# The logits' PSUM bank joins the pool of all products: eight shared banks in place of seven and one

## The chip, the cores and the metric

The kernel runs on one core of a Trainium2 chip. The metric is device time in microseconds (us). The engines are TensorE (PE; its weight loads are PEld), VectorE (DVE), ScalarE (ACT), GpSimd (POOL) and SyncE (SP), which issues most DMAs. Products of TensorE land in PSUM, which has eight banks of 128 partitions by 512 float32 words; DVE or ACT reads them out.

## What is computed

Two layers, one behind the other, in float32. The first mixes 8 batches of 2496 tokens of 256 channels by a filter in the frequency domain; the second sends each token to one of 8 experts.

```python
X = np.fft.rfft(x, axis=1)                      # x: 8 x 2496 x 256
y = np.fft.irfft(X * (filt_r + 1j * filt_i)[None], n=2496, axis=1)
x = y.reshape(19968, 256)
logits = x @ w_gate                             # 8 experts
expert_idx = np.argmax(logits, axis=1)
probs = softmax(logits); gate_w = probs[np.arange(N), expert_idx]
for e in range(8):                              # the rows of expert e
    h = np.maximum(x_sorted[lo:hi] @ w1[e], 0.0)     # 256 -> 1024
    y_sorted[lo:hi] = h @ w2[e]                      # 1024 -> 256
out = gate_w[:, None] * y_sorted[inv_perm]
```

## The kernel before

**The transform.** A sequence of 2496 = 39 x 64 tokens is transformed by small matrices. For each batch `stage_a` (table `tas`, tile `fin` into `zo`, stored to `zd`) makes the transform of length 39; `stage_b` (table `tbs`) that of length 64, with the filter applied on DVE while the product is read: into `ys` by one multiplication, into `yw` by two of half the partitions, all three reading the bank; then `ys` and `yw` are added, on DVE or POOL. `stage_c` (table `tcs`, from `ys` into `uo`, stored to `ud`) and `stage_d` (table `tds`, from `fin` loaded out of `ud`, into `yo`) go back. Batch 0 keeps its intermediate values on the chip (`first_a`, `turn_z`, `first_c`, `turn_u`).

**The logits.** The rows of `yo` are turned (`turn_y`), multiplied by the gate weights into the PSUM tile `lt`, and copied out into `ls`. Batches 0 to 2 do this in `logits`, up to eight rows of tokens at a time, and turn the result back in `turn_logits`; batches 3 to 7 do it in `block_logits`, with blocks of 32 channels, and `block_back`. A side stream, `route`, then finds expert and place of each token with small DVE instructions, and POOL scatters the rows to DRAM (`rows`); `tile_map` decides which tile of rows belongs to which expert.

**The experts.** Tiles of 512, 256 or 128 rows are loaded (`xg`), turned on DVE (`xT`), multiplied by `w1t` into `hT` and by `w2t` (or `w2s`, weights that stay) into the result `ys`, which POOL scatters to the output. Large tiles use products "by quarters": sums of blocks (`sums`, `wsum`, `hsum`, `tsum`) with seven products in place of eight, whose results DVE adds into `hT` as it reads the banks; ACT applies the ReLU.

**PSUM.** All products but the logits' ask `bank()` for a tile in the pool `ps` with seven banks. The logits' tile `lt` has a pool of its own, `psr`, with one bank, which is part of the transform's set of pools (`fft`) and is given up with it, when the last batch has been routed; nothing opens a PSUM pool after that.

**The order of the work.** The order of instructions is decided when the program is built, by `Order`: it keeps a clock for every engine (`t["tensor"]` and so on), with estimates for each operation, the times at which tiles are done (`ready`) and at which buffers come free (`Slots.free`). The main loop takes the next step for TensorE from the open steps of the transform (`wait_of`) and from two streams of expert products (`when`), and prefers what it holds to be startable within 0.2 us. Both ask for a free bank:

```python
banks = ps.free("bank") if f[3] < 0.9 else max(ps.free("bank"), ps.free("bank", 1) - 0.85)
return max(0.0, max(nc.ready(*needs), banks) - t["tensor"])
```

`ps.free("bank", 1)` is the time at which a second bank comes free. Steps of logits ask in this way too, though `lt` lies in the other pool. Which bank a product gets is decided by the same clock, since `ps` is marked as live: `tile` takes the one that is freed first by the plan. `either` gives a read of a bank to DVE or ACT, whichever ends it first by the plan. Loads and stores are issued on SP when the plan's TensorE clock has reached their time (`more_loads`, `flush`, `prefetch`). On the chip, each instruction waits by semaphores for what it really needs, in the order that the plan has set for its engine.

Of the kernel before, what the change touches and what calls it, by code (L numbers as in the profile page):

```python
# [10 lines left out]
F32 = mybir.dt.float32  # L11
# [5 lines left out]
PSUM = bass.MemoryType.PSUM  # L17
DRAM = bass.MemoryType.DRAM

P = 128  # L20
S = 2496
D = 256
E = 8
# [9 lines left out]
NG = 22  # L33
TP = NB * N1
# [5 lines left out]
CT = 32  # L40
# [253 lines left out]
def kernel(  # L294
# [19 lines left out]
    def open_pool(stack, name, bufs, **named):  # L314
        return nc.pool(stack.enter_context(tc.tile_pool(name=name, bufs=bufs, **named)), bufs)
# [9 lines left out]
    for b in range(B):  # L325
        GROUPS.append([])
        for rows, most in WANT[b]:
            n = min(most, max(0, ((b + 1) * S - (N - left) - E * (rows - 1)) // rows))
# [22 lines left out]
    tau0 = perm.tile([1, 32], F32, name="tau0")  # L351
    prow = perm.tile([P, 1], I32, name="prow")
    need = perm.tile([1, 1], I32, name="need")
    ps = open_pool(ctx, name="ps", bufs=7, space=PSUM)

    fft = ctx.enter_context(ExitStack())
    cst = open_pool(fft, name="cst", bufs=1)
    sb = open_pool(fft, name="sb", bufs=2)
    psr = open_pool(fft, name="psr", bufs=1, space=PSUM)

    tas = cst.tile([TP, TK], F32, name="tas")
    tbs = cst.tile([P, P], F32, name="tbs")
# [33 lines left out]
    def bank():  # L396
        return ps.tile([P, 512], F32, tag="bank", name="bank")
# [12 lines left out]
    def evac(o, i, n):  # L410
        either(i, n, lambda: nc.vector.tensor_copy(o, i), lambda: nc.scalar.copy(out=o, in_=i))
# [281 lines left out]
    def block_logits(b, c):  # L693

        n = CH[c][1]
        yt = yts.pop((b, c))
        lt = psr.tile([P, 2, E * NG], F32, tag="lt", name="lt").rearrange("p i w -> p (i w)")[:, :n * CT]
        for r in range(2):
            for q in range(4):
                j = 4 * r + q  # L700
                mm(lt[q * CT:(q + 1) * CT], lhsT=wb[:, j, :], rhs=yt[:, :, j * CT:(j + 1) * CT], start=(r == 0), stop=(r == 1))
        ls = outs["s", b, c] = sb.tile([P, 4 * CT], F32, tag="ls", name="ls", bufs=1)[:, :n * CT]
        evac(ls, lt, n * CT)
# [8 lines left out]
    def logits(b, g):  # L712

        js = range(min(4, NG // 2 - 4 * g))
        w = len(js) * CT
        both = [yts.pop((b, c)) for c in range(2 * g, min(2 * g + 2, len(CH)))]
        pair = [both[j // 2][:, j % 2].rearrange("p (i h) q -> p i h q", i=2) for j in js]
        lt = psr.tile([P, 2, E * NG], F32, tag="lt", name="lt")[:, :, :TP]
        for dh in range(DH):
            for j in js:  # L720
                mm(lt[j * CT:(j + 1) * CT], lhsT=wg[:, dh, :], rhs=pair[j][:, :, dh, :],
                   start=(dh == 0), stop=(dh == DH - 1))
        ls = sb.tile([P, 4, D], F32, tag="yt", name="ls")[:, :2, :TP]
        evac(ls[:w], lt[:w], 2 * TP)
        outs["l", b] = (g, w, ls)
# [849 lines left out]
```

## Time and profile before

| | |
|---|---|
| median of 3 runs | 1476.66 us (1476.07 to 1478.16) |
| profiled execution | 1478.19 us, span 1476.5 us |
| mean granted clock of TensorE | 0.995 |
| bytes moved by DMA | 278.19 MB, 188 GB/s in the mean |

The profile is of one execution. Its span goes from the first to the last instruction of the program; the execution's own time is 1.7 us longer. A group of instructions is named by output and inputs, `bank<-ys,tcs`, with the buffers' numbers left out, so all banks of `ps` are `bank`. All lines are L246, since a helper issues everything. A wait is put down to the instruction that released it.

### The profile page before, as it was taken

The page shows a single profiled execution, that of the slowest core. Times are in us where ns is not written, and L with a number is a line of the kernel's source. Part 1 is how long each engine was busy: PE and PEld are TensorE (multiplying, and loading weights), DVE is VectorE, ACT ScalarE, POOL GpSimd, SP SyncE. Part 2 cuts the span into 40 slices and gives each one's busy share as a digit, 9 for nine tenths or more (in the row PEclk, how much of TensorE's full clock was granted, in tenths as well). Part 3 has the DMA queues.
Part 4 walks back from the last instruction along what each step waited for, and adds up shares of the span by engine and source line. Part 5 has one row for each costly group of instructions (what it writes and reads, how often), then busy time and mean ns, then how long its engine had stood idle before and what let it go on. Part 6 is the DMA issues. An engine that isn't in the chain of part 4 may idle for free.

```text
span 1476.5 us, 25693 instructions
## 1 busy us (share of the span) xinstructions
PE 1440.1 (98%) x7828; PEld 1147.0 (78%) x7828; DVE 848.7 (57%) x1819; ACT 480.6 (33%) x1004; POOL 822.0 (56%) x1213
## 2 busy tenths in 40 slices
PE   8998998999999999999999999999999999999998
PEld 6543656877677777776787778879999998999997
DVE  4667579235866675457665465567878775431110
ACT  4554452333332232322222232223232322223332
POOL 4434445635555654655465656858989878831111
PEclk9999999999999999999999999999999999999999
DMA  9759889795985585556544735556655425456661
GB/s 269 230 193 340 280 291 299 253 258 185 321 206 167 172 260 151 131 162 229 156 119 132 214 93 148 153 177 188 173 173 167 133 71 137 135 189 176 174 190 43
DMA packets 216383, 278.19 MB, mean 188 GB/s; under 512 B 124131, under 2 KB 163708, under 8 KB 216245
## 3 DMA queue, kind: packets, MB, share of 16 engines
q1 hardware_dynamic: 197125, 233.19, 53.2%
q0 software_dynamic: 19120, 43.33, 8.4%
q8 instruction: 66, 1.08, 0.3%
q14 instruction: 72, 0.59, 0.1%
HBM read 196.45 MB, written 80.64 MB: 188 GB/s over the span
## 4 chain that ended last, share of the span: by engine, by line
PE 85%; DVE 6%; DMA 4%; issue 3%; ACT 1%; POOL 0%; SPq 0%; DVEq 0%; POOLq 0%; ACTq 0%
PE bank L246 83%; DMA fin<-in_x_dram 2%; PE lt L246 2%; DVE hT L246 1%; DVE yw L246 1%; DVE ys L246 1%; DMA fin<-ud 1%; DMA fin<-zd 1%; DMA zd<-zo 1%; POOL out_dram L246 0%; DVE take L246 0%; ACT hT L246 0%; SPq L246 0%; DMA w1t<-in_moe_w_dram 0%; DMA xg<-rows 0%
## 5 line engine op out<-in xcount | busy, mean ns | idle before, releaser
L246 DVE TENSOR_TENSOR hT<-bank,hT 128x512 f32<-128x512 f32 (+1 forms) x504 | 301.9, 626 | 181.4 <-PE bank L246 101.2
L246 PE MATMUL bank<-w2t,hT 128*128 128x256 f32 (+1 forms) x1984 | 388.6, 350 | 1.6 <-DVE hT L246 1.6
L246 PEld LDWEIGHTS bank<-w2t,hT 128*128 128x128 f32 x1984 | 334.5, 190 | 49.9 <-issue 9.6
L246 PE MATMUL bank<-xT,w1t 128*128 128x256 f32 (+1 forms) x1728 | 314.9, 328 | 0.3 <-DVE hT L246 0.3
L246 POOL DMA_INDIRECT out_dram<-ys,ng x161 | 160.0, 994 | 252.5 <-ACT ys L246 121.5
L246 PEld LDWEIGHTS bank<-xT,w1t 128*128 128x128 f32 x1728 | 264.6, 191 | 33.1 <-issue 9.9
L246 ACT ACTIVATE hT<-hT 128x1024 f32<-128x1024 f32 (+1 forms) x144 | 135.5, 960 | 399.8 <-DVE hT L246 387.4
L246 POOL DMA_INDIRECT rows<-yo,row x176 | 181.9, 1033 | 70.8 <-POOL yo L246 31.3
L246 ACT ACTIVATE ys<-bank,ng 128x256 f32<-128x256 f32 x102 | 48.4, 475 | 287.4 <-PE bank L246 231.7
L246 PE MATMUL bank<-sums,wsum 128*128 128x256 f32 (+1 forms) x576 | 135.7, 358 | 1.5 <-DVE hT L246 1.5
L246 PE MATMUL bank<-w2s,hT 128*128 x592 | 132.9, 380 | 1.3 <-ACT hT L246 1.3
L246 POOL TENSOR_TENSOR wsum<-w1t 128x256 f32<-128x256 f32 x72 | 60.1, 835 | 114.5 <-PE bank L246 96.7
L246 PEld LDWEIGHTS bank<-w2s,hT 128*128 128x128 f32 x592 | 110.2, 190 | 15.8 <-ACT hT L246 2.0
L246 PEld LDWEIGHTS bank<-sums,wsum 128*128 128x128 f32 x576 | 100.3, 190 | 21.6 <-issue 11.3
L246 DVE STREAM_TRANSPOSE xT<-xg 128x512 f32<-128x512 f32 (+2 forms) x126 | 57.5, 494 | 57.7 <-PE bank L246 56.9
L246 PE MATMUL bank<-ys,tcs 128*128 128x512 f32 x140 | 73.8, 613 | 7.6 <-DVE yw L246 4.2
L246 DVE TENSOR_TENSOR ys<-bank,ht 128x512 f32<-128x512 f32 x80 | 54.9, 686 | 44.3 <-PE bank L246 38.0
L246 PE MATMUL bank<-fin,tds 120*128 120x512 f32 (+1 forms) x168 | 77.1, 580 | 3.1 <-DMA fin<-ud 2.6
L246 PE MATMUL bank<-fin,tas 117*120 117x512 f32 x154 | 75.5, 608 | 4.2 <-DMA fin<-in_x_dram 3.3
L246 PE MATMUL bank<-fin,tbs 128*128 128x512 f32 x140 | 72.7, 607 | 2.3 <-DMA fin<-zd 2.2
L246 ACT ACTIVATE hT<-bank 128x128 f32<-128x128 f32 (+1 forms) x191 | 57.2, 303 | 53.9 <-PE bank L246 45.3
L246 PE MATMUL bank<-xT,wsum 128*128 128x256 f32 (+1 forms) x288 | 68.8, 362 | 1.1 <-DVE yw L246 0.9
(171 smaller groups left out, 1778.9 us busy)
## 6 DMA issues: line engine op xcount, KB each, us to landing
w1t<-in_moe_w_dram SPq DMA_DIRECT2D x126, 512.0 KB
w2t<-in_moe_w_dram SPq DMA_DIRECT2D x68, 512.0 KB
fin<-in_x_dram SPq DMA_DIRECT2D x39, 512.0 KB
fin<-zd SPq DMA_DIRECT2D x35, 512.0 KB
ud<-uo SPq DMA_DIRECT2D x35, 512.0 KB
fin<-ud SPq DMA_DIRECT2D x35, 512.0 KB
zd<-zo SPq DMA_DIRECT2D x35, 480.0 KB
xg<-rows SPq DMA_DIRECT2D x112, 128.0 KB
```

What stands on the lines that cost most here:

```text
L246: return real(*args, **named)
```

## The change

The pool `ps` gets eight banks. The pool `psr` is dropped, and both logits functions take their tile from `bank()`. In `logits` the two halves of the tile now begin 256 words apart in place of 176.

```diff
-    ps = open_pool(ctx, name="ps", bufs=7, space=PSUM)
+    ps = open_pool(ctx, name="ps", bufs=8, space=PSUM)
...
-    psr = open_pool(fft, name="psr", bufs=1, space=PSUM)
...
-        lt = psr.tile([P, 2, E * NG], F32, tag="lt", name="lt").rearrange("p i w -> p (i w)")[:, :n * CT]
+        lt = bank()[:, :n * CT]
...
-        lt = psr.tile([P, 2, E * NG], F32, tag="lt", name="lt")[:, :, :TP]
+        lt = bank().rearrange("p (i w) -> p i w", i=2)[:, :, :TP]
```

## Prediction

> **What bounds the kernel now.** I read the page's first part, then windows by stage, then the waits of TensorE (PE), then the timeline around its longest wait.
>
> ```profile
> PE 1440.1 (98%) x7828; PEld 1147.0 (78%) x7828; DVE 848.7 (57%) x1819; ACT 480.6 (33%) x1004; POOL 822.0 (56%) x1213
> ```
>
> TensorE is busy for 1440.1 of 1476.5 us. The change alters no product in number or size, so what can be won is mostly the 36.4 us in which it stands. 1.5 us of them lie ahead of its first matmul and 6.5 after its last. The windows (length, then busy time of PE, PEld, DVE, ACT, POOL, then clock, DMA share and GB/s) tell where the other 28.4 are:
>
> ```profile
> 20.30:240.00 219.70, 205.64 (x870) 114.10 (x870) 152.29 (x355) 104.59 (x223) 102.71 (x143) 0.97 0.82 268
> 240.00:892.00 652.00, 645.19 (x3169) 489.06 (x3168) 387.15 (x847) 200.55 (x401) 359.23 (x572) 1.00 0.64 193
> 892.00:985.00 93.00, 89.38 (x429) 77.66 (x430) 59.86 (x153) 23.57 (x41) 61.37 (x98) 1.00 0.52 142
> 985.00:1280.00 295.00, 293.10 (x1988) 274.73 (x1987) 207.91 (x333) 83.39 (x137) 248.41 (x300) 1.00 0.52 152
> 1280.00:1470.00 190.00, 190.00 (x1273) 177.78 (x1271) 34.43 (x110) 60.42 (x187) 44.66 (x79) 1.00 0.53 157
> ```
>
> Half (14.1) stands in the first stage, where DMA is at 0.82 and DVE at 69%; 6.8 in the long mixed stage; 3.6 where the last batch is routed; 1.9 in the expert tail; and nothing after 1280 us. What ended the waits of TensorE:
>
> ```profile
> PE bank L246 <- DVE yw L246: 5.1, 3, 3.4
> PE bank L246 <- DVE hT L246: 3.9, 5, 1.6
> PE bank L246 <- DVE ys L246: 3.4, 3, 1.6
> PE bank L246 <- DMA fin<-in_x_dram: 3.3, 2, 2.4
> PE bank L246 <- ACT hT L246: 2.7, 7, 0.5
> ```
>
> Columns: total us, times, longest. Which are waits for a **bank**? No matmul reads yw, and it is the last reader of the bank of a `stage_b` product: 5.1 us are bank waits. The five on DVE hT are held by `sums`, `wsum` and `w2t` matmuls whose inputs had other writers last (the w2 product reads hT only after its ReLU on ACT); each release is an addition that read a bank: 3.9. Of the ACT ones, three (0.55 at 174.8, 0.45 at 511.1, 0.44 at 695.6 us) stand before DFT matmuls, which read no hT: 1.4. The other four wait for hT itself, as data. So banks cost 5.1 + 3.9 + 1.4 = **10.4 us in 11 waits**. The `DVE ys` 3.4 are data (`stage_c` reads ys), and the DMA waits (3.3 here, with 2.6 on fin<-ud and 2.2 on fin<-zd further down the view: 8.1) don't ask for a bank either.
>
> The longest of them, in the timeline of TensorE and of DVE:
>
> ```profile
> 232.31 1.03 PE L246 MATMUL bank<-sums,w1t 128*128 128x256 f32 x4
> 234.07 1.12 PE L246 MATMUL bank<-ys,tcs 128*128 128x512 f32 x2 [0.74 <-DVE yw L246]
> 238.64 1.97 PE L246 MATMUL bank<-ys,tcs 128*128 128x512 f32 x2 [3.44 <-DVE yw L246]
> ...
> 236.50 0.68 DVE L246 TENSOR_TENSOR ys<-bank,ht 128x512 f32<-128x512 f32 x1
> 237.20 0.69 DVE L246 SCALAR_TENSOR_TENSOR yw<-bank,ht 64x512 f32<-64x512 f32 x1
> 237.90 0.68 DVE L246 TENSOR_TENSOR yw<-bank,ht 64x512 f32<-64x512 f32 x1
> ```
>
> DVE is behind: it holds banks with frequency products (three reads of 0.69 us each, then one addition), and between two of them runs 1.9 us of small routing instructions. TensorE stands until 238.59, when the last `yw` read ends. The clock record then shows half speed from 238.8 to 242.2 us.
>
> **What the Trainium skill says.** "PSUM — Partial Sum Buffer", Specifications: eight banks of 2 KiB per partition. Seven and one are thus all, and the change only shares the eighth; its tile of 352 words needs a bank in either case. "Perfetto Trace Analysis", Matmul Optimizations, says to make all eight banks work so that more can overlap. The trace agrees only in size: with seven, bank waits are 10.4 of 1476.5 us. "TensorE: Matmul & The Clock Gate", What's actually happening: after an idle window of about 3.4 us the clock halves until a busy one has passed. The trace has three such spells (3.4, 6.8 and 3.4 us at half); the last follows the 3.44 us wait and costs about 3.4 x 0.5 = 1.7 us.
>
> **The change, part by part.** (1) *What is added*: a place for an eighth product. The tile lt is written by 39 logits products. Summed from first matmul to the end of the copy, the old bank is held for 67.8 us, between 75.7 and 892.5 us: 8% of that stretch, and never in the tail. At none of the 11 waits is lt held. The pool therefore really gains 0.92 of a bank in the mixed stages and one in the tail.
>
> (2) *What that is worth in the present order.* An extra bank doesn't make DVE faster. It lets TensorE go on by one product, then it waits for the same release. So an episode of waiting shrinks by the smaller of its wait and one product's time. A tcs, tas or tds product takes 0.43 us (two tcs started 0.43 apart before the next kind at 226.7 and 227.13), a product by quarters 0.86 (starts at 229.72 and 230.58). Episodes: 174.8: 0.43; 234 to 239 (two waits, one backlog): 0.43; 511.1: 0.43; 687.6 (a wait of 0.91): 0.86; 695.6: 0.43; 859.7: 0.26; 979.9 and 983.5 (1.48 and 1.62, one backlog): 0.86; 1222.7: 0.44; 1237.3: 0.15. Sum: **4.3 us**. Bounds: 0, if each freed product only meets the next wait; 10.4 plus the 1.7 of clock = 12.1, if none of these waits is left.
>
> (3) *What logits lose.* They now can wait for a bank that DVE holds. In this trace the one wait in front of lt (1.0 us) is for its data. A logits product already is released by the planner only when a bank of the other pool is due, so I take 0; were all 39 to meet bank waits at their present share (10.4 in 1476 us, over the 67.8 us held), it is 0.5 us. No instruction, copy or DMA is added; the strides inside lt (256 in place of 176 words between the halves) change no count of columns: 0.
>
> (4) *The order itself.* It is written by `Order`, greedily: `ps.free("bank")` enters `wait_of` and `when`, and `bank()` takes the bank with the earliest planned release. An eighth makes some step eligible earlier, and from there on the order, the choice of DVE or ACT in `either`, and when SP issues loads all differ. SP's loads and stores go out by the planned TensorE time, so they move along with it; the cover for that is the DMA share, 0.82 up to 240 us (poor) and 0.5 to 0.6 later (good). The trace can't price this. I bound it by the idle time that it can rearrange outside banks: DMA 8.1 and data 3.4 + 1.3 = 12.8 us; half of that either way, 6 us, and I take 0 as its middle.
>
> Sum: 1478.19 (the profiled execution, span 1476.5) - 4.3 = 1473.9. That execution lies 1.5 above the median of 1476.66, so the median becomes 1472.4, and I say **1472**.
>
> **Rivals.** *It only moves the waits* (1476.5; between 1473.7 and 1479.6). For it: in 204 to 239 us the chain of waits runs along DVE, almost without TensorE; a backlog is bounded by the slow engine, whatever the number of banks. Against it: most of the nine episodes are shorter than the product that could fill them.
>
> *Running further ahead makes DVE's queue later* (slower). With one more product in flight, one more evacuation stands in DVE's in-order queue before those that TensorE needs as data: the ys sums, the hT additions that ReLU waits for. Its price is one frequency product on DVE, 3 x 0.69 = 2.1 us, each time that such data is what ends TensorE's wait. It decides from the third such place (4.3 / 2.1). At four places, with one more half-clock spell: 8.4 + 1.7 - 4.3 = +5.8, so 1482.5. For it: DVE ys already ends 3.4 us of waits, and 69% DVE load before 240 us leaves little to catch up with. Against: after 240 us DVE is at 59%, with idle time that a longer queue would use up first.
>
> *All bank waits go and the new order also hides half of the DMA waits*: 12.1 + 4.0 = 16, so 1460.5. For it: the largest waits sit in few places. Against: the DMA ones end transfers on a nearly full bus.
>
> That the change does nothing is not possible in the tail: seven banks there are all that the program can name today. That it does less than a bank is the first rival.
>
> **How the numbers follow.** A measurement of this kernel can tell about 0.2% (3 us) from no change. Forecast (1468 to 1473.7): 0.42. Large gain: 0.13. Only moved: 0.22. Slower: 0.23. Faster is 0.42 + 0.13 = 0.55, within 0.2% 0.22, slower 0.23. The range leaves out half of the large-gain case and half of the slower one: 1462 to 1482. As faster and slower cases both count, the forecast's own range is 1468 to 1473.7.
>
> **What would show it.** Right: TensorE's busy time unchanged near 1440 (a little less if the half-clock spell near 239 us is gone); waits of PE on DVE yw, DVE hT and on ACT before DFT matmuls falling from 10.4 to about 6; nothing gained after 1280 us. Step 3 is wrong if lt waits on DVE or ACT releases by over 0.5 us in sum. The first rival: the same total, in other places. The slower one: waits of `bank<-ys,tcs` on DVE ys and of w2 products on hT above 5 us together, or a fourth half-clock spell. Step 4 is wrong if DMA waits move by more than 6 us. The forecast as a whole is wrong if the gain comes from somewhere else than idle TensorE time.

## The result, and the profile after

The changed kernel took 1469.72 us in the median of 11 runs, beside 1477.11 us for the kernel before; the ratio is 0.9949 (95% interval 0.9935 to 0.9962), some 7.5 us. A second comparison gave 0.9943 (0.9927 to 0.9959). The forecast was 1472 with a range of 1462 to 1482. Its direction and its order of size held. Its reason did not: in the order that it reasoned about, no gain from the eighth bank is seen (e1 below, 1.0007), and another order gains as much without it (n_before_hop, 0.9940).

The profiled execution took 1474.50 us (span 1472.8), the slowest of its 11, so its sum is not the median's. Its first part, busy time and share of each engine:

```profile
PE 1438.4 (98%) x7828; PEld 1148.5 (78%) x7828; DVE 835.8 (57%) x1818; ACT 480.5 (33%) x1005; POOL 818.9 (56%) x1214
```

TensorE does the same 7828 matmuls in 1438.4 us (1440.1 before). The windows by stage, columns as before:

```profile
20.30:240.00 219.70, 205.76 (x863) 114.43 (x864) 145.43 (x340) 104.87 (x224) 100.39 (x138) 0.96 0.81 258
240.00:892.00 652.00, 642.39 (x3163) 488.44 (x3162) 394.04 (x876) 200.84 (x407) 365.89 (x580) 1.00 0.65 196
892.00:985.00 93.00, 93.00 (x448) 81.38 (x447) 57.13 (x145) 23.46 (x37) 63.47 (x97) 1.00 0.54 157
985.00:1280.00 295.00, 294.73 (x2001) 276.75 (x2000) 200.38 (x334) 84.09 (x137) 242.69 (x302) 1.00 0.52 151
```

The 3.6 us in which TensorE stood between 892 and 985 us are gone, and the 1.9 after that are 0.3. Between 240 and 892 us TensorE stands for 9.6 us in place of 6.8, since the longest bank wait, which ended at 238.6 us before, now lies in this window. What ended its waits, over the whole span:

```profile
PE bank L246 <- DMA fin<-in_x_dram: 8.6, 4, 2.9
PE bank L246 <- DMA fin<-zd: 5.4, 3, 2.4
PE bank L246 <- DVE yw L246: 3.4, 1, 3.4
PE bank L246 <- DMA fin<-ud: 3.3, 2, 2.0
PE bank L246 <- DVE hT L246: 2.0, 3, 1.4
...
PE bank L246 <- ACT hT L246: 1.2, 2, 0.8
```

By the prediction's way of counting, bank waits are 3.4 on yw, 2.0 on DVE hT, 0.4 of the ACT hT ones (in front of `rx,sel`, which reads no hT) and 0.4 on ACT yo and uo: 6.2 us in place of 10.4, and 6.2 once more in the second profile of the changed kernel. The DMA waits are 17.3 us in place of 8.1, 14.9 of them before 240 us, where the order is still almost wholly that of the kernel before. This is for the most part a difference between executions: the kernel before, profiled once more (e0 below), had 11.7 us of them, and e3, with the same order up to the tail, 6.7.

So the stretch that can be compared begins with the last logits of batch 2 (at 220.4 us before, 227.9 after). From there to the last matmul it is 1249.6 us before and 1238.4 after. The orders part a moment later, at the two `ys,tcs` matmuls at 234.07 us, just where the kernel before runs into its longest bank wait; the changed kernel puts a product by quarters ahead of them and then waits as long:

```profile
240.65 1.03 PE L246 MATMUL bank<-xT,wsum 128*128 128x256 f32 x4
241.51 1.02 PE L246 MATMUL bank<-ys,tcs 128*128 128x512 f32 x2
245.97 1.13 PE L246 MATMUL bank<-ys,tcs 128*128 128x512 f32 x2 [3.43 <-DVE yw L246]
```

### The profile page after: what moved, and what is told of

Its sections match the earlier page's. It is cut to its first block, busy times and chain, and to the rows that moved or that the text cites. A ratio compares the mean times of both kernels' runs of the same rounds, so it can differ in the third digit from the quotient of the medians.

```text
span 1472.8 us, 25703 instructions
## 1 busy us (share of the span) xinstructions
PE 1438.4 (98%) x7828; PEld 1148.5 (78%) x7828; DVE 835.8 (57%) x1818; ACT 480.5 (33%) x1005; POOL 818.9 (56%) x1214
## 4 chain that ended last, share of the span: by engine, by line
PE 85%; DMA 6%; DVE 4%; issue 2%; POOL 1%; SPq 1%; ACT 1%; POOLq 0%; DVEq 0%; ACTq 0%
PE bank L246 85%; DMA fin<-in_x_dram 2%; DMA fin<-ud 2%; DVE yw L246 1%; DVE ys L246 1%; DMA ud<-uo 1%; DMA fin<-zd 1%; SPq L246 1%; POOL out_dram L246 0%; DVE hT L246 0%; DMA w1t<-in_moe_w_dram 0%; DMA ng<-rows 0%; ACT hT L246 0%; DMA zd<-zo 0%; DMA xg<-rows 0%
## 5 line engine op out<-in xcount | busy, mean ns | idle before, releaser
L246 PEld LDWEIGHTS bank<-w2t,hT 128*128 128x128 f32 x1984 | 335.1, 190 | 53.0 <-issue 11.7
L246 POOL TENSOR_TENSOR wsum<-w1t 128x256 f32<-128x256 f32 x72 | 56.5, 785 | 82.2 <-PE bank L246 57.7
```

Source lines behind the costliest of these rows:

```text
L246: return real(*args, **named)
```

## The experiments

The change does two things: it gives products an eighth bank, and it makes the planner write another order. Theory A: the bank makes the gain. Theory B: the order does. Theory C: waits only move.

**Bank and order apart (e1, e2).** A tile is planned in one set of banks (`plan`) and given one of another (`given`). Every engine's list of instructions in e1 is that of the kernel before, and in e2 that of the changed kernel. The experiments use the code of the change with this added, shortened here:

```diff
-            k = min(range(n), key=lambda k: self.freed(past[k], tag))
+            pick = lambda among, of: min(among, key=lambda k: self.freed(of[k], tag))
+            k = pick(self.plan[lt] if self.plan else range(n), past)
             name = past[k]
-            named.update(tag=f"{tag}{k}", bufs=1)
+            at = pick(self.given[lt], self.held) if self.plan else k
+            named.update(tag=f"{tag}{at}", bufs=1)
...
+    A = {False: range(8), True: range(8)}       # shared by all
+    B = {False: range(7), True: [7]}            # the logits apart (lt=True)
+    ps.plan, ps.given = B, A                    # e1;  A, B in e2
```

> The planner's clock works with seven banks and one, so every engine's instructions stand in the order of the kernel before; only the bank that each product is given comes from all eight, the one freed first by the same clock. Theory A (the bank itself: TensorE waits less for evacuations in the order that it has): about 4.3 us less than before (1472 to 1474), which is over half of the measured gain, and bank waits of TensorE falling from 10.4 to about 6 us. Theory B (the other order, which the planner writes once it counts eight banks, makes the gain): within 1.5 us of before. Theory C (only moved: a backlog of VectorE holds the eighth bank too): no change, and the bank waits keep their sum in the same places.

Measured: 1476.18 us in the median, ratio 1.0007 (0.9995 to 1.0018). In the old order no gain from the eighth bank is seen: the interval goes from 0.7 us less to 2.7 us more. Yet the waits fell. In the profile of e1 the wait at 980 to 984 us of before (1.48 + 1.62) is 0.60 + 1.83, the 0.91 at 687.6 is gone, and all of TensorE's standing after the last logits of batch 2 is 12.3 us, against 16.5 before and 16.0 in e0. Between 600 and 1100 us its waits are these, some of those of before first, then those of e1:

```profile
PE bank L246 <- DVE hT L246: 3.4, 3, 1.6
...
PE bank L246 <- DVE ys L246: 1.1, 1, 1.1
...
PE bank L246 <- DVE yw L246: 0.9, 1, 0.9
PE bank L246 <- ACT hT L246: 0.4, 1, 0.4
```

```profile
PE bank L246 <- ACT hT L246: 2.3, 2, 1.8
PE bank L246 <- DVE yt L246: 1.2, 1, 1.2
PE bank L246 <- DVE ys L246: 1.1, 1, 1.1
PE bank L246 <- DVE hT L246: 0.6, 1, 0.6
PE bank L246 <- DVE oe L246: 0.4, 1, 0.4
```

DVE hT has fallen from 3.4 us in the same stretch of before to 0.6, yw from 0.9 to nothing; ACT hT has risen from 0.4 to 2.3, of which 1.8 is one wait of a w2 product for the ReLU's data. That is theory C at that place. In sum the prediction's 4.3 us were nearly seen as less standing (16.5 - 12.3 = 4.2), and didn't shorten the run. The profiled execution is one of the slower ones (1480.92 us) and lost time in the clock: after the first stage it ran 13.6 us at half speed, before and e0 only 3.4, which costs it up to 5.1 us (half of the difference).

> The reverse: the planner counts eight, so every engine's instructions stand in the order of the changed kernel, but products are given only seven banks and the logits the eighth. Theory A: most of the gain is lost, 1473 to 1477 us. Theory B: the gain stays, 1468 to 1471 us. If both add, about 3 us less than before, and with e1 the two differences sum to the 7.4 us of the whole change.

Measured: 1473.76 us, ratio 0.9989 (0.9975 to 1.0003). The new order with the old banks keeps little of the gain, if any. The profiled execution (1469.88 us) is faster than the median, with a first stage of only 219.3 us; the stretch after it took 1242.4 us, against 1238.4 and 1239.1 in the two profiles of the changed kernel. In the same order TensorE waits for 9.6 us on evacuations (yw, DVE hT, ACT hT and ACT uo) in place of the 6.2 counted above.

```profile
PE bank L246 <- DVE hT L246: 4.1, 5, 2.2
PE bank L246 <- DVE yw L246: 4.0, 2, 3.4
...
PE bank L246 <- ACT hT L246: 0.9, 2, 0.4
PE bank L246 <- ACT uo L246: 0.6, 2, 0.4
```

Neither part alone makes the gain, so neither A nor B was enough at this point.

**Stages apart (e3, e4).** The sets change when the transform's pools are closed:

```diff
+    ps.plan = ps.given = B                      # e3;  A in e4
...
                 fft.close()
+                ps.plan = ps.given = A          # e3;  B in e4
```

> Seven banks and one, for planner and products, until the transform's pools are closed at about 890 us; from there on eight for both. Prediction's step 2: the tail's share is 0.86 + 0.44 + 0.15 = 1.5 us less than before. If the tail's bank waits of 3.7 us (979.9, 983.5, 1222.7 and 1237.3 us) go as a whole, 3.7 us less. Theory C: no change.

Measured: 1476.81 us, ratio 1.0015 (0.9997 to 1.0033). No gain from the tail's bank is seen. TensorE's order changes there at only 16 of its 7828 matmuls.

> Eight banks shared with the logits, for planner and products, until the transform's pools are closed; after that seven. If the gain is made in the mixed stage, about 6 us less than before (all but the tail's 1.5); if it is made in the tail, within 2 us of before. With e3 the two differences should sum to about 7.4 us.

Measured: 1471.44 us, ratio 0.9967 (0.9955 to 0.9979). Eight banks up to 890 us bring most of the gain; the rest, 0.002, is within the intervals of the two comparisons.

**Is the order a draw (r_after, e0, n_before_hop, n_after_hop)?** A greedy plan answers any small change with another order. If the order of before is just a poor one, a change of a number that means nothing for the banks should do as well.

```diff
-    HOP = 0.1
+    HOP = 0.11      # n_before_hop: in the kernel before; n_after_hop: in the changed one
```

> The changed kernel once more, on the chip of the next three. Its ratio to before should lie near 0.995 (0.9935 to 0.9962 was measured). Its second profile shows how far the stages of one execution vary: from the start to the last logits of batch 2 (about 228 us in the first profile) the order is that of the kernel before, so this stretch should vary with the DMA alone, and the rest should again be some 7 to 11 us shorter than in the profile of before (1249.6 us).

Measured: ratio 0.9943 (0.9927 to 0.9959). The stretch from the last logits of batch 2 took 1239.1 us (1238.4 in the first profile); the stretch ahead of it 223.0 (227.9).

> Control: the kernel before, with the code of the order-and-bank experiments (seven banks and one for planner and products; order of all engines as before). All theories: 1.000, within 0.0015. Its profile is a second one of the kernel before: if the stretch from the last logits of batch 2 on is again near 1249.6 us, stage times of single profiles can be compared to 2 us; if it is near 1244, they can't.

Measured: 1.0010 (0.9996 to 1.0023); the stretch took 1247.8 us. e3, whose order and banks are those of before up to 890 us, took 1243.8 for it. The stretch can be cut at the 4451st matmul, near 955 us: on either side of it TensorE has the same matmuls in every order run here. The part up to there took 735.3, 735.0 and 733.8 us (before, e0, e3), the rest 514.2 and 512.8, and 510.1 in e3 with its eight banks. So with the same order and banks single profiles differ by some 2 us in either part.

> Seven banks and one, as before, with one number of the planner (its estimate of a semaphore's way, HOP) 0.11 in place of 0.10 us: an order as different from before as that of the changed kernel, without a bank more. Theory L (the gain is a draw: any other order differs by some us): 0.995 to 1.005, as likely on either side. Theory P (eight banks, counted by the planner and given to products, are what brings it): at or above before, 0.999 to 1.005.

Measured: 1469.08 us, ratio **0.9940** (0.9920 to 0.9960): the whole gain, with seven banks and one.

> Eight shared banks, as in the changed kernel, with HOP 0.11: another order again. Theory L: anywhere from 0.992 to 1.003, not tied to 0.995. Theory P: 0.993 to 0.997, as in the changed kernel, since the banks and the plan that counts on them are kept.

Measured: 1471.73 us, ratio 0.9951 (0.9935 to 0.9967). Theory P falls by n_before_hop; theory L stands for seven banks, and the eight-bank orders lie where that seven-bank one does.

**Two more orders, and bank against order once more (n_before_res, n_after_res, e6, e7).**

```diff
-    RESERVE = 60.0
+    RESERVE = 62.0  # n_before_res, n_after_res
...
-    HOP = 0.1
+    HOP = 0.11      # e6: plan B, given A;  e7: plan A, given B
```

> Seven banks and one, with another number of the planner changed by little (RESERVE 62 in place of 60 us): a third order for the banks of before. Theory L (an order is a draw, and the order of before is a poor one): most likely below before, 0.992 to 1.000. If seven and one are worse than eight in themselves: 0.998 to 1.004, and n_before_hop (0.994) was the exception.

Measured: 1470.22 us, ratio 0.9964 (0.9946 to 0.9983).

> Eight shared banks with RESERVE 62: a third order for the banks of the changed kernel. Theory L: 0.992 to 1.000, with no tie to 0.995. If eight banks hold the gain whatever the order: 0.993 to 0.997, as twice before.

Measured: 1469.56 us, ratio 0.9960 (0.9945 to 0.9974).

> The order of n_before_hop (planned with seven and one), but products are given all eight banks. In a good order an eighth bank may be worth what TensorE still waits for banks: its profile shows yw 2.9 and ACT hT 1.6 us. Theory A2 (the bank helps a good order): 0.991 to 0.993. Theory L (only the order counts, as in e1): 0.994, as without it.

Measured: 1467.46 us, ratio 0.9934 (0.9916 to 0.9952). It has the lowest ratio of all kernels run here; its interval takes in the ratios of n_before_hop and of the changed kernel, so it is not shown to be better than either.

> The order of n_after_hop (planned with eight), but products are given seven and the logits one. e2 did this for the changed kernel's order and lost all but 0.001 of its 0.0055. If that holds for orders that count on eight banks in general: 0.998 to 1.000. If e2's loss was its own: 0.995 to 0.997.

Measured: 1474.58 us, ratio 0.9987 (0.9974 to 1.0000). As in e2, the banks taken away from an order that was planned with them cost it most of its gain.

All of it in one table (ratios to the kernel before):

| order planned with | given seven and one | given eight |
|---|---|---|
| seven and one: that of before | 1 (control 1.0010) | 1.0007 |
| seven and one: HOP 0.11 | 0.9940 | 0.9934 |
| seven and one: RESERVE 62 | 0.9964 | |
| eight: the change | 0.9989 | 0.9949, 0.9943 |
| eight: HOP 0.11 | 0.9987 | 0.9951 |
| eight: RESERVE 62 | | 0.9960 |

Five other orders, each on the banks that it was planned for, lie between 0.9940 and 0.9964, two with seven banks and three with eight. (e4, with the change's order up to the tail, has 0.9967.) The order of before is the one that lies apart. That HOP 0.11 and RESERVE 62 are simply better estimates is not seen: with eight banks they gave 0.9951 and 0.9960, no more than the change. An eighth bank given to an order planned without it changes 0.0003 to 0.0006 against its own control, measured in another comparison, which is nothing within the intervals; taken from an order planned with it, it costs 0.0040 (0.9989 over 0.9949) and 0.0036, about 5.5 us.

Part of what the order of before loses is seen between 600 and 1100 us, where neither the first stage's DMA nor the half clock of its beginning plays a part. The windows of that stretch, in this order: before, e0 and e1 (order of before), the changed kernel and its second profile, n_before_hop and e6 (the order of HOP 0.11, planned with seven), and last e2 and e7, from which a bank was taken.

```profile
600.00:1100.00 500.00, 491.64 (x2656) 406.88 (x2656) 315.77 (x638) 140.93 (x251) 327.19 (x464) 1.00 0.55 160
600.00:1100.00 500.00, 492.90 (x2658) 407.31 (x2657) 316.07 (x638) 140.60 (x250) 327.35 (x465) 1.00 0.55 160
600.00:1100.00 500.00, 494.44 (x2646) 408.19 (x2646) 316.42 (x639) 140.70 (x249) 327.07 (x466) 1.00 0.55 160
...
600.00:1100.00 500.00, 497.58 (x2683) 415.91 (x2682) 312.92 (x646) 140.62 (x250) 325.98 (x467) 1.00 0.55 162
600.00:1100.00 500.00, 497.23 (x2693) 416.60 (x2692) 316.24 (x650) 140.87 (x249) 323.52 (x464) 1.00 0.56 163
...
600.00:1100.00 500.00, 498.47 (x2697) 415.70 (x2696) 319.81 (x652) 143.40 (x252) 325.75 (x465) 1.00 0.56 163
600.00:1100.00 500.00, 499.70 (x2708) 417.86 (x2705) 321.44 (x655) 144.18 (x253) 327.58 (x466) 1.00 0.56 163
...
600.00:1100.00 500.00, 496.90 (x2691) 416.01 (x2690) 315.96 (x650) 141.71 (x250) 324.58 (x464) 1.00 0.55 163
600.00:1100.00 500.00, 496.43 (x2686) 414.61 (x2685) 317.76 (x657) 137.84 (x240) 323.67 (x468) 1.00 0.55 163
```

TensorE stands for 8.4, 7.1 and 5.6 us in the order of before, 2.4 and 2.8 in that of the change, 1.5 and 0.3 in the third. In the ten profiles of other orders it is never above 4.1, and in the four of the order of before (e3: 6.2) never below 5.6. It is not the whole account: e2 and e7 stand for only 3.1 and 3.6 us there, and gain next to nothing. These are waits of the order of before in this stretch:

```profile
685.62 1.10 PE L246 MATMUL bank<-ys,tcs 128*128 128x512 f32 x2 [1.11 <-DVE ys L246]
687.62 1.10 PE L246 MATMUL bank<-xT,wsum 128*128 128x256 f32 x4 [0.91 <-DVE yw L246]
...
979.92 1.10 PE L246 MATMUL bank<-sums,wsum 128*128 128x256 f32 x4 [1.48 <-DVE hT L246]
...
983.50 1.78 PE L246 MATMUL bank<-w2t,hT 128*128 128x256 f32 x7 [1.62 <-DVE hT L246]
```

e0 has all four of them again, within 0.01 us of these lengths. Of the second pair e1 has 0.60 and 1.83 and e3 0.61 and 1.61, both with eight banks there. This pair stands where DVE runs the many small instructions of the last `tile_map`. It does not decide: n_before_res meets both waits again, at its own place, and has 0.9964 all the same; n_before_hop, with the same order of TensorE from 955 us on, meets neither.

```profile
974.65 1.10 PE L246 MATMUL bank<-sums,wsum 128*128 128x256 f32 x4 [1.47 <-DVE hT L246]
...
978.23 3.72 PE L246 MATMUL bank<-w2t,hT 128*128 128x256 f32 x16 [1.61 <-DVE hT L246]
```

The two parts of the stretch after the last logits of batch 2, cut at the 4451st matmul, show the loss as a whole (us, one execution each; the four other orders are n_before_hop, n_before_res, n_after_hop and n_after_res):

| | order of before | order of the change | other orders |
|---|---|---|---|
| up to 955 us, banks as planned | 735.3, 735.0 (e0), 733.8 (e3) | 730.6, 730.9, 730.6 (e4) | 728.0, 726.3, 726.8, 726.7 |
| with other banks | 736.9 (e1) | 733.7 (e2) | 725.2 (e6), 730.1 (e7) |
| the rest, banks as planned | 514.2, 512.8 (e0), 510.1 (e3) | 507.7, 508.2, 509.1 (e4) | 509.0, 511.0, 509.4, 509.9 |
| with other banks | 510.1 (e1) | 508.8 (e2) | 507.9 (e6), 509.4 (e7) |

In the first part the order of before is the slowest, whatever its banks, though e2 comes within 0.1 us of its fastest profile; e2 and e7 lose some 3 us there against their own orders with eight. No single wait accounts for this.

## Why the prediction was right, and where not

*What bounds the kernel.* Right in the main: TensorE's matmuls are unchanged, and most of the gain is standing time. After the last logits of batch 2 the two profiles differ by 11.2 us; 6.6 of them are standing (16.5 to 9.9), and 4.6 are busy time of the same matmuls, for which no cause is shown. Bank waits were to fall from 10.4 to about 6; they fell to 6.2. The five windows that the prediction shows hold 26.4 of its 28.4 us of standing; the other 2.0 lie before 20.3 us.

*Step 1, a place more.* Right as a count.

*Step 2, the worth of the bank in the present order: 4.3 us.* This is the step that failed. e1 measures it alone: 1.0007, between 0.7 us less and 2.7 us more. Its mechanics can be seen in the one profile, with 4.2 us less standing after the first stage, but the runs were no shorter. Part of it lies in the clock: the mean granted clock of e1's 22 runs is 0.9925, that of before in the same comparison 0.9933, and 0.0008 of 1475 us at half speed is 2.4 us of such time, at most 1.2 us of loss. The rest isn't settled. One lead is the first stage: up to the last logits of batch 2 it takes 223.0 to 228.2 us in the seven profiles with eight banks given, and 216.7 to 224.2 in the seven with seven. But the profiled executions lie 1.8 us above the medians of their kernels in the former and 2.6 below in the latter (means), so this need not hold for the runs as a whole. The prediction saw "it only moves the waits" as a rival to the whole change; for this step it fits better than the gain that was forecast.

*Step 3, logits lose nothing.* Right: no matmul that writes lt waits for an evacuation in the profile after.

*Step 4, the order, taken as 0 within 6 us either way.* This is the term that was the result. Moving from the order of before to another gives 0.9940 and 0.9964 with seven banks, that is 5 to 9 us. The prediction treated a new order as noise with its middle at 0. That would be so from an average order; the one of before turns out to be poor, and the five other orders, on their own banks, all gained. Nothing in the one profile could tell that, but rewriting the order by a number of no weight could have.

Sum: predicted 4.3 from the bank and 0 from the order; measured, for the old order, 0 from the bank. For the eight-bank orders the two can't be split into a sum: order alone 0.9989, bank alone 1.0007, both 0.9949. That the forecast lay close is therefore luck: the term that made up all of it gave nothing where it was worked out, and the term put at 0 held the gain. A likely reason for the loss in e2 and e7 is that the plan picks its steps believing that eight products can be in flight, and with seven each comes up against a bank still being read. The bank waits fit that: in the same order 9.6 us in e2 against 6.2, and by the same count 5.5 in e7 against 2.0 in n_after_hop. That the plan's belief is the reason, no experiment shows by itself.

*The slower rival.* It did not come. Its place, data waits on DVE ys before `ys,tcs`, is 0.7 us in the profile after (3.4 before). A fourth half-clock spell did appear in the first profile after, at 155 us, where the order is unchanged.

*DMA waits.* The prediction's own test called step 4 wrong if these moved by more than 6 us. They moved by 9.2, but e0 shows 3.6 of movement with nothing changed, and 14.9 of the 17.3 us lie before the orders part: the test was badly chosen.

The Trainium skill ("Perfetto Trace Analysis", Matmul Optimizations) advises to use all eight banks. No run here contradicts using them; but given to a fixed order that lacked one, the eighth shows no gain (1.0007 and, in the other seven-bank order, 0.9934 against 0.9940).

## What to carry to other kernels

Where a program plans its own order, a change of a resource is two changes: the resource, and a new order. Before the gain is put down to the resource, rewrite the order a few times with numbers that shouldn't matter, and run the old order with the new resource. If the redraws gain as much as the change, the old order was a poor draw, and trying a few orders is an improvement by itself. An order that was planned with the resource may still need it: here it lost 0.0036 to 0.0040 without.

## What had not been expected of the hardware

The clock halved after less standing than the prediction took from "TensorE: Matmul & The Clock Gate", What's actually happening (an idle window of about 3.4 us). In e1 it fell after waits of 0.4 and 1.2 us within two microseconds. The windows before and during the spell:

```profile
867.70:871.20 3.50, 1.93 (x18) 1.37 (x20) 3.40 (x7) 1.80 (x4) 0.55 (x1) 0.99 0.00 0
871.20:874.60 3.40, 3.40 (x23) 2.48 (x14) 3.12 (x8) 0.76 (x6) 2.82 (x4) 0.50 0.45 92
```

TensorE was busy for 1.93 of the 3.5 us ahead of the spell, which then lasted 3.4 us. The two executions e3 and e0 have the same pair of waits at this place (0.48 and 1.03 us). In e3 a spell follows, in e0 none does, though TensorE was busy for 1.99 of the 3.5 us ahead in both (e3 first, then e0):

```profile
855.90:859.40 3.50, 1.99 (x25) 1.25 (x23) 3.40 (x8) 1.80 (x6) 0.30 (x1) 0.99 0.00 0
859.40:862.80 3.40, 3.40 (x12) 2.74 (x9) 3.12 (x8) 0.43 (x4) 2.82 (x4) 0.50 0.55 111
...
865.30:868.80 3.50, 1.99 (x15) 1.38 (x17) 3.40 (x8) 1.82 (x4) 0.84 (x2) 1.00 0.00 0
868.80:872.20 3.40, 3.40 (x29) 2.89 (x30) 3.16 (x7) 0.97 (x6) 2.76 (x4) 1.00 0.34 72
```

So equal waits can bring a spell in one execution and not in another; what decides is not shown here.
